# A second level of seven products for M4, stored weight sums, and merged down sums in an FNet and GeGLU kernel

## The chip, the cores and the metric

The kernel runs on one core of a Trainium2 chip. The metric is the device time of one execution in microseconds (us). Three runs of the kernel before gave 794.04, 794.16 and 794.77 us, a median of 794.16.

## What is computed

The input x has 2048 tokens of 512 features. It is normalised (layer norm), and two branches and the input are added:

```python
xn = layernorm(x)
# branch A: FNet, the real part of a 2-D DFT by matrices
a = xn @ dft_hid_re.T ; b = xn @ dft_hid_im.T
A = dft_seq_re @ a - dft_seq_im @ b
# branch B: gated GeGLU, 512 -> 1792 -> 512
B = (gelu(xn @ w_gate) * (xn @ w_up)) @ w_down
out = x + A + B
```

All of it is float32. A float32 matmul is made of three matmuls of a faster type (fp32r): each operand is split into a high part (a rounded copy, on ScalarE) and a low part (the difference, on VectorE), and high times high, low times high and high times low are added in PSUM (`mm3`). So every operand costs one ScalarE and one VectorE operation, the "split".

## The kernel before

Branch A and the preparation of the operands fill the time up to about 380 us (the first product of unit 0 starts at 379.8) and are not touched; the last products of branch A are fillers in the first units. Branch B is worked on in 28 *units* n. Even units make the gate of a block of 256 hidden features, odd units its up projection. Units 0 to 13 take the first half of the tokens (1024), units 14 to 27 the second half with the same weights, so weight block n and weight block n + 14 are the same. I call them the first and the second pass.

**Seven products.** A unit's product, weights (512 x 256) by tokens (512 x 1024), is split into two by two blocks and computed with seven block products in place of eight (the Strassen-Winograd scheme). They are numbered r = 0 to 6; product 0 is M1, product 4 is M4. Product r needs a sum of weight blocks or a plain block (`wl[n, r]`) and the same of token blocks (`xT[pass, r, i]`, i the two halves of the contraction). The weight sums are four VectorE operations on half tiles per unit (`weight_sums`, line 847), their splits are `weight_split`: three full tiles and a half. Each product is two `mm3`, six matmuls of 128 x 128 by 512 (`product`, `mult`). A unit uses three PSUM banks: a (products 0 and 1), b (5, 6, 3) and c (4, 2), with copies of intermediate sums between them: a to b, b to q6, b to w (`copy`, line 1993), and c added to w and q6 (`sums`, line 1997). PSUM has eight banks of this size.

**A second level for product 0.** From unit 4 on, product 0 of the units n and n + 1 (n even: 4, 6, 8, 10, 12) is computed for both passes at once: two weight blocks, two token halves and two halves of the contraction are again two by two blocks, so seven inner products of three matmuls each (`inner`, `inner_p`) give the four results. Those of the first pass go on in their units. Those of the second pass are completed in side tiles (q2, w2), written to DRAM by POOL (`m_park`), and loaded again in the second pass, where ScalarE copies them into the banks a and b in place of product 0 (`fetched`, the seeds sa and sb). The inner products need their own sums of tokens (`inner_x`, four once) and of weights (`inner_w`, four quarter operations per pair, line 911).

**Down projection.** Two units make one block q of hidden features (14 in all, 7 per pass): gelu of the gate, times the up projection, four tiles; four more sums (`h_sum`) and seven splits prepare them for the down projection, which is also done with seven products (`down_product`, per product r and output half j three matmuls per block). Blocks are taken in *turns*: in each pass first one block, then two, two and two. After a turn's product, ScalarE copies the bank to a tile `part` (line 2034) and POOL adds that tile onto `partial` in DRAM with an accumulating DMA (line 2036). A turn has 14 such steps (seven products, two halves). They are spread over the units as fillers: `fill` puts one at the fixed places d(0) to d(3) in a unit's order of products, and PE works on them while the copies of the unit are made. Just before the last blocks, two of the seven sums are added in SBUF by VectorE instead (line 2027). The very last turn (blocks 12 and 13) is `last_down`, an order written by hand that runs after everything else: it takes the parked sums as seeds in PSUM, adds the last products, combines them and stores.

**Operands of the second pass.** The tokens of the second half are prepared (sums and splits, `sum_x`, `xT_split`) while units 2 to 13 run, at units given by `X_UNIT`; seven of the resulting pairs of tiles (`PARK`) are written to DRAM and fetched later, to save SBUF.

**The order of the work.** Units 2 to 27 are ordered by a planner (`Plan`), a list scheduler that runs when the kernel is built: every operation is added with its engine, a cost (V5 = .6, V2 = .333 for VectorE on a full and a half tile, A5 = .52 and A2 = .31 for ScalarE, MM = .2267 per matmul), what it comes after, the tiles that it makes and uses, and the banks that it holds. PE's order is the order in which products are added. From PE's clock every other operation gets a due time, and then each engine takes what can start first. Loads on SP start at most `FETCH_AHEAD` = 16 before they are due, and operations that make tiles at most `EARLY` = 16. SBUF is 109 slots of 128 x 512 float32, of which the planner uses 107. Each engine, and the DMA queues of SP and POOL, then work strictly in that order, each instruction waiting for its operands.

Of the kernel before, what the change touches and what calls it, by code (L numbers as in the profile page):

```python
# [14 lines left out]
P = 128  # L15
S = 2048
D = 512
# [19 lines left out]
class Plan:  # L37
# [6 lines left out]
    def __init__(self, clocks, live, cap, ahead, early=LATE):  # L44
        self.early, self.had = early, set()
# [9 lines left out]
    def add(self, name, engine, cost, fn, after=(), makes=(), uses=(), due=None, mb=0, banks=(), holds=(), adds=False, begin=0.):  # L55
# [5 lines left out]
        self.ops[name] = dict(e=engine, cost=cost, fn=fn, after=after, makes=dict(makes), due=due, mb=mb, adds=adds, begin=begin, banks=tuple(banks), drains=bool(holds) and engine != "p")  # L61
# [48 lines left out]
    def choose(self, ready, frees, spare):  # L110
        best = None
        for e, names in ready.items():
            able = []
            for n, at in names.items():
                o = self.ops[n]
                at = max(at, self.clock[e], o["begin"])
                if e == "s":
                    at = max(at, o["due"] - self.ahead)
                elif o["makes"] and not o["begin"]:
                    at = max(at, o["due"] - self.early)  # L120
# [110 lines left out]
def fnet_geglu_kernel(ctx: ExitStack, tc: tile.TileContext, x, xt, cs, dh, wgu, wd, out):  # L231
# [81 lines left out]
    m_park = dram.tile([NP, P, CH], F32, name="m_park")  # L313
# [542 lines left out]
    def weight_split(n, k):  # L856

        if k == 3 or (k == 0 and fetched(n)):
            p, src = (3, wx[n][3][:, 0]) if k else (1, wx[n][0][:, 1])
            wl[n, p] = hl_half("w")  # L860
            return wl[n, p], src
# [20 lines left out]
    LEAD = 4  # L882

    def lead(n):
        return n % 2 == 0 and LEAD <= n < NP

    def fetched(n):
        return isinstance(n, int) and n >= NP + LEAD

    m0, xi, wi = {}, {}, {}  # L890

    def inner_x(k):

        b11, b21 = (xr[0, i, 0] for i in range(2))
        b12, b22 = (xr[1, i, 0] for i in range(2))
        u, v = {6: (b22, b12), 4: (b12, b11), 5: (b22, xi.get(4)), 3: (b21, xi.get(5))}[k]
        xi[k] = slot("xi")
        nc.vector.tensor_sub(xi[k], u, v)

    def inner_xsplit(k):  # L900
        xi["hl", k] = hl_tile(f"xi{k}")
        return xi["hl", k], xi[k]

    def inner_w(n, k):

        a, b = (wx[m][0][:, 0] for m in (n, n + 1))
        if k == 0:
            wi[n] = slot("wi", F32, (P, 4, P))
        op, u, v = ((OP.add, b[:, :P], b[:, P:]), (OP.subtract, wi[n][:, 0], a[:, :P]), (OP.subtract, a[:, :P], b[:, :P]),
                    (OP.subtract, a[:, P:], wi[n][:, 1]))[k]  # L910
        nc.vector.tensor_tensor(wi[n][:, k], u, v, op=op)

    def inner_wsplit(n):
        wi["hl", n] = slot("wih", F32R, (P, 4, P)), slot("wil", F32R, (P, 4, P))
        return wi["hl", n], wi.pop(n)

    def inner(n, k, ps, first=False):

        if k in (0, 1):
            a, b = [t[:, cols(k)] for t in wl[n, 0]], xT[0, 0, k]  # L920
        elif k == 3:
            a, b = [t[:, cols(1)] for t in wl[n + 1, 0]], xi["hl", 3]
        else:
            a, b = [t[:, {4: 0, 5: 1, 6: 2, 2: 3}[k]] for t in wi["hl", n]], xi["hl", k] if k != 2 else xT[1, 0, 1]
        mm3(ps, a, slice(P), b, first, True, resumed=not first)
# [78 lines left out]

    def last_down(qs):


        sp = NC // 2 - 1
        bank, p0 = {}, {}

        def add(dst, r, j, blk=None):
            nc.vector.tensor_add(dst, bank[r, j], dst)
            if blk:
                store(sp, blk[0], j, blk[1], dst)

        steps = [(r, j) for r in D_ORDER for j in range(2)][:-1]
        halves = [slice(h * HD, (h + 1) * HD) for h in range(2)]
        todo = steps + [(3, 1, h) for h in range(2)]

        def seed():  # L1020
            if todo:
                r, j, *h = k = todo.pop(0)
                sl = halves[h[0]] if h else slice(CH)
                bank[k] = ps_tile("dn")[:, :HD if h else CH]
                nc.scalar.activation(bank[k], acc[r, j][:, sl], AF.Copy)

        seed()
        seed()
        yield
        while carry:  # L1030
            carry.pop(0)()
        seed()
        for k in range(4):
            h_sum(NP - 1, k)
        seed()
        parts = [h_split(NP - 1, k) for k in (1, 0, 2, 3)]
        for r, j in steps:
            ps = bank[r, j]
            down_product(qs, r, j, ps, True)
            if r == 0:  # L1040
                p0[j] = slot("p0")
                nc.scalar.activation(p0[j], ps, AF.Copy)
            elif r == 2:
                nc.scalar.activation(acc[2, j], ps, AF.Copy)
            elif r == 1:
                nc.vector.tensor_add(acc[1, j], ps, p0[j])
                store(sp, 0, j, 0, acc[1, j])
            elif r == 5:
                add(p0[j], 5, j)
                nc.vector.tensor_add(acc[2, j], acc[2, j], p0[j])  # L1050
            elif r == 4:
                add(acc[2, j], 4, j, (0, 1))
            elif r == 6:
                add(p0[j], 6, j)
                nc.vector.tensor_add(acc[4, j], bank[4, j], p0[j])
                store(sp, 1, j, 1, acc[4, j])
            elif r == 3:
                add(p0[j], 3, j, (1, 0))
            seed()
            if parts and (r, j) != steps[0]:  # L1060
                split(*parts.pop(0))
        for h, (sl, queue) in enumerate(zip(halves, (nc.scalar, nc.sync))):
            down_product(qs, 3, 1, bank[3, 1, h], True, sl)
            nc.vector.tensor_add(p0[1][:, sl], bank[3, 1, h], p0[1][:, sl])
            queue.dma_start(out[3, 2 * sp, :, sl], p0[1][:, sl])
# [79 lines left out]
    def unit(n):  # L1145
# [49 lines left out]
        if fetched(n):  # L1195
            for t in (b, a):
                nc.scalar.activation(t, m0[n], AF.Copy)
        else:
            multiply(0, a, True)
            nc.scalar.activation(b, a, AF.Copy)  # L1200
# [624 lines left out]
    EARLY = 16  # L1825
    FETCH_AHEAD = 16
    PARK = [(0, 0), *((k, i) for k in (1, 4, 5) for i in range(2))]

    def middle():

        plan = Plan(dict(p=.3, v=6.6, a=4.2, s=0., g=0.), 84, SLOTS - 2, FETCH_AHEAD, EARLY)
        plan.idle = [0.] * 5 + [1., 1.5, 2.]
        add, W = plan.add, 6 * MM
# [6 lines left out]
        def split_of(key, f, ready, uses, makes, wide=True, **kw):  # L1840
# [5 lines left out]
            add(("lo", key), "v", V5 if wide else V2, lambda: split_lo(*begun.pop(key)), after=[("hi", key)], uses=[*uses, *makes])  # L1846

        def weights(m, load=True, sums=True, splits=True):
            if load:
# [389 lines left out]
```

## Time and profile before

| | |
|---|---|
| median of three runs | 794.16 us |
| the profiled execution's own time | 794.38 us |
| its span, first to last instruction | 792.6 us |
| PE, share of the span | 99%, 3468 matmuls |
| VectorE (DVE) | 92% |
| ScalarE (ACT) | 67% |
| GpSimd (POOL) | 21% |
| unit 2 begins | 404.7 us |
| unit 14 begins (second pass) | 583.1 us |
| last product of unit 27 ends | 769.6 us |

The profile is one execution. PE is TensorE's matmuls, PEld its weight loads, DVE VectorE, ACT ScalarE, POOL GpSimd and SP the engine that issues most DMAs (SPq is its queue). A row of a group gives line, engine, operation, output and inputs with their shapes, how often (x), then busy time in us and the mean in ns, then the idle time of the engine in front of it and who ended it. A row of waits gives the waiting engine and line, the releaser, the sum in us, how often, and the longest. A row of the chain gives start, length and what ran.

### The profile page before, as it was taken

To read this page: it belongs to the slowest core of one execution; us is meant where nothing else is said; L and a number is where in the kernel's file an instruction comes from. 1 tells how busy PE (TensorE), PEld (TensorE's weight loads), DVE (VectorE), ACT (ScalarE), POOL (GpSimd) and SP (SyncE) were. 2 spreads that over 40 slices of the span, in tenths; PEclk is the share of its full clock that TensorE was granted. 3 is DMA by queue.
4 is the path that set the end of the run, shared out by engine and by line. 5 is a ranking of instruction groups with operands and counts; after the bars stand their busy time and mean duration, and the time that the engine had idled before them with its cause. 6 is when DMAs were issued, how large, how long until landed. Compare 5 with 4: busy or idle time off the path is not lost.

```text
span 792.6 us, 11549 instructions
## 1 busy us (share of the span) xinstructions
PE 787.7 (99%) x3468; PEld 648.7 (82%) x3468; DVE 731.9 (92%) x1364; ACT 534.4 (67%) x1016; POOL 168.2 (21%) x242
## 2 busy tenths in 40 slices
PE   9999999999999999999999999999999999999998
PEld 6888888888888888888878888888888888888886
DVE  7999999999899979899999798999898889889897
ACT  6997656556534656366666876686876788777774
POOL 0110520044211231000202522422222234202220
PEclk9999999999999999999999999999999999999999
DMA  9967997879998897778725985966987799958972
GB/s 325 378 175 223 346 355 256 271 263 316 357 336 312 310 290 289 245 267 296 195 67 72 256 150 94 260 113 99 284 233 156 196 183 228 283 127 201 218 146 107
DMA packets 96432, 183.78 MB, mean 232 GB/s; under 512 B 11217, under 2 KB 18929, under 8 KB 96177
## 3 DMA queue, kind: packets, MB, share of 16 engines
q1 hardware_dynamic: 69840, 120.89, 44.9%
q0 software_dynamic: 26240, 61.88, 36.2%
q8 instruction: 27, 0.44, 0.2%
q14 instruction: 37, 0.29, 0.1%
q10 hardware_dynamic: 288, 0.26, 0.1%
HBM read 118.23 MB, written 67.91 MB: 235 GB/s over the span
## 4 chain that ended last, share of the span: by engine, by line
PE 90%; DVE 6%; DMA 1%; ACT 1%; issue 1%; ACTq 0%; DVEq 0%
PE m L280 33%; PE dn L280 17%; PE b L280 15%; PE c L280 10%; PE y L280 6%; PE a L280 5%; PE z L280 4%; DVE wl L269 1%; DVE ws L847 1%; DVE xr L780 1%; DMA dl<-d_park 1%; DMA wd<-in_wd 0%; DVE xr L781 0%; DMA x<-in_x 0%; DVE psl L269 0%
## 5 line engine op out<-in xcount | busy, mean ns | idle before, releaser
L264 ACT ACTIVATE psh<-pan 128x512 fp32r<-128x512 f32 x203 | 115.4, 625 | 72.4 <-DVE pan L660 26.4
L269 DVE TENSOR_TENSOR psl<-pan,psh 128x512 fp32r<-128x512 f32 x198 | 127.8, 684 | 8.9 <-ACT psh L264 8.2
L2036 POOL DMA_DIRECT2D partial<-part x94 | 81.8, 893 | 217.2 <-ACT part L2034 165.0
L280 PE MATMUL m<-psh,xcl 128*128 128x512 f32 x232 | 90.3, 389 | 0.0
L280 PE MATMUL m<-psl,xch 128*128 128x512 f32 x232 | 90.3, 389 | 0.0
L280 PE MATMUL m<-psh,xch 128*128 128x512 f32 x232 | 90.3, 389 | 0.0
L2034 ACT ACTIVATE part<-dn 128x512 f32<-128x512 f32 x94 | 55.2, 597 | 35.6 <-PE dn L280 33.1
L269 DVE TENSOR_TENSOR wl<-ws,wh 128x512 fp32r<-128x512 f32 x84 | 56.7, 685 | 3.1 <-ACT wh L264 3.0
L264 ACT ACTIVATE wh<-ws 128x512 fp32r<-128x512 f32 x84 | 51.1, 625 | 4.4 <-DVE ws L847 4.1
L280 PEld LDWEIGHTS m<-psh,xcl 128*128 128x128 f32 x232 | 43.5, 188 | 9.1
L280 PEld LDWEIGHTS m<-psl,xch 128*128 128x128 f32 x232 | 43.6, 188 | 9.0
L280 PEld LDWEIGHTS m<-psh,xch 128*128 128x128 f32 x232 | 43.6, 188 | 9.0
L581 POOL DMA_DIRECT2D partial<-part x28 | 21.0, 803 | 111.6 <-DMA bst<-mean_rstd 61.9
L269 DVE TENSOR_TENSOR htl<-s,hth 128x512 fp32r<-128x512 f32 x56 | 37.4, 686 | 3.3 <-ACT hth L264 3.1
L280 PE MATMUL m<-psh,xa 128*128 128x512 f32 x116 | 40.4, 389 | 0.0
L653 DVE TENSOR_TENSOR pan<-pan 128x512 f32<-128x512 f32 x58 | 37.9, 682 | 0.0
L957 DVE TENSOR_TENSOR s<-s 128x512 f32<-128x512 f32 x56 | 36.8, 685 | 0.1
L264 ACT ACTIVATE hth<-s 128x512 fp32r<-128x512 f32 x56 | 33.9, 625 | 2.6 <-DVE s L957 2.5
L280 PE MATMUL dn<-hl,wh 128*128 128x512 f32 x84 | 32.8, 390 | 0.0
L280 PE MATMUL dn<-hh,wh 128*128 128x512 f32 x84 | 32.7, 389 | 0.0
L280 PE MATMUL dn<-hth,wh 128*128 128x512 f32 x84 | 32.7, 389 | 0.0
L280 PE MATMUL dn<-hth,wl 128*128 128x512 f32 x84 | 32.7, 389 | 0.0
(850 smaller groups left out, 2317.9 us busy)
## 6 DMA issues: line engine op xcount, KB each, us to landing
pan<-in_cs SPq DMA_DIRECT2D x157, 256.0 KB, 5.4
partial<-part POOLq DMA_DIRECT2D x122, 256.0 KB, 5.4
wx<-in_wgu SPq DMA_DIRECT2D x56, 256.0 KB, 4.4
t_park<-pan POOLq DMA_DIRECT2D x29, 256.0 KB, 5.5
pan<-t_park SPq DMA_DIRECT2D x29, 256.0 KB, 4.5
wd<-in_wd SPq DMA_DIRECT2D x28, 256.0 KB, 5.2
acc<-partial SPq DMA_DIRECT2D x28, 256.0 KB, 5.3
zr<-z_park SPq DMA_DIRECT2D x16, 256.0 KB, 3.6
```

What stands on the lines that cost most here:

```text
L264: nc.scalar.activation(t[0], src, AF.Copy, scale=float(sign))
L269: engine.tensor_sub(t[1], src, hi)
L280: nc.tensor.matmul(ps, a[u][:, sl], b[v], start=first and r == 0, stop=last and r == 2, skip_group_check=resumed)
L581: nc.gpsimd.dma_start(partial[sp, r, j], ypart.pop((r, j)), **({} if r in (0, 5, 6) else {"accum_op": OP.add}))
L653: return [lambda: nc.vector.tensor_sub(t3, b22, b12), lambda: nc.vector.tensor_sub(t1, b12, b11), lambda: (nc.vector.tensor_sub(b22, *((t1 ...
L780: nc.vector.tensor_sub(v, v, xst[sp, t, 0])
L847: nc.vector.tensor_tensor(r[k][:, h], u, v, op=op)
L957: nc.vector.tensor_sub(t, u, v)
L2034: nc.scalar.activation(part[0], tiles[j], AF.Copy)
L2036: add(("da", qs[-1], r, j), "g", .6, lambda j=j, part=part: nc.gpsimd.dma_start(partial[sp, r, j], part[0], accum_op=OP.add), after=[("dc" ...
```

## The change

- **M4.** Product 4 gets the second level too, for the four pairs that begin with units 6, 8, 10 and 12 (`LEAD = {0: 4, 4: 6}`). The functions of the inner level take the outer product r (0 or 4) as a parameter. In units 20 to 27 bank c is seeded by a third ScalarE copy. Two more banks are held in a pair unit. Both lists of inner token sums start two units ahead (`INNER_AHEAD`).
- **Weight sums stored.** Units 4 to 13 write their two tiles of weight sums to DRAM (`ws_park`, on POOL). Units 18 to 27 load them (`load_sums`) instead of computing them, and load only the two half tiles of raw weights that are products themselves (`load_short`), as one tile whose split is one operation. From unit 20 on, the half that product 4 would need is neither loaded nor split.
- **Turns.** The turns are `TURNS`: one block, then pairs through blocks 9 and 10, and three for the last turn (11, 12, 13), so the second pass has turns of 2, 2 and 3 in place of 1, 2, 2 and 2. Block 7 goes with block 8, and all 14 steps of a turn are taken one half at a time. Steps are spread evenly over the units up to the next turn (`wanted`).
- **The last turn** is added to the planner, step by step, in place of the hand-written order.
- **Order and settings.** A unit's order of products is given by a string (digits are products, d0 to d3 fillers, X and Y inner products of this and the pair before). Look-ahead: 28 for operations that make tiles, 22 for loads, 12 for raw weights before unit 12. Two input sums of the second half (k = 6 and 3) are also written to DRAM and read back (`x_park`), the splits of k = 2 are added to `PARK` and half of k = 4 taken out, and the units of the splits change.

```diff
-    LEAD = 4
+    LEAD = {0: 4, 4: 6}
+    LATER = {0: False, 4: False}
+    KEEP_SUMS = (4, NP)
...
+    def short(n):
+        return fetched(n, 0) and n >= NP + KEEP_SUMS[0]
+
+    def half_split(n, k):
+        return k == 3 or (k < 2 and fetched(n, 4 * k) and not (k == 0 and short(n)))
...
-    EARLY = 16
-    FETCH_AHEAD = 16
-    PARK = [(0, 0), *((k, i) for k in (1, 4, 5) for i in range(2))]
+    HURRY = 28
+    LOOSE = 15
+    LATER_HURRY = 28
+    FETCH_AHEAD = 22
+    W_AHEAD = 12
+    TURNS = [[0], [1, 2], [3, 4], [5, 6], [7, 8], [9, 10], [11, 12, 13]]
+    INNER_AHEAD = 2
+    INTO_ACC = (6, 3)
+    SUMS_AT = 3.5
+    PARK = [(0, 0), (4, 0), *((k, i) for k in (1, 5, 2) for i in range(2))]
...
+            if sums and at >= count + keep:
+                add(("sw", m, 3), "s", .9, lambda: load_sums(m, at - count, int(name == "d")), after=[("lw", m), ("pw", name, at - count)],
+                    mb=2 * MB if name or not fetched(m, 4) else 1.5 * MB, makes={("ws", m, 0): 1, ("ws", m, 1): 1}, uses=[("wx", m)])
+            elif sums:
                 box = []
+                if keep <= at < count:
+                    add(("pw", name, at), "g", 1.2, lambda: park_sums(m, at, int(name == "d")),
+                        after=[("sw", m, 3)], uses=[("ws", m, 0), ("ws", m, 1)], mb=2 * MB)
...
+        def park_sums(m, at, d):
+            for i in range(2):
+                nc.gpsimd.dma_start(ws_park[d, at, i], wx[m][1 + i].rearrange("p a b -> p (a b)"))
+
+        def load_sums(m, at, d):
+            t = [slot("ws", F32, (P, 2, HD)) for _ in range(2)]
+            for i in range(2):
+                some = slice(1 - i if fetched(m, 4) else 0, 2)
+                nc.sync.dma_start(t[i][:, some], ws_park[d, at, i].rearrange("p (a b) -> p a b", a=2)[:, some])
+            wx[m] = (wx[m][0], *t, wx[m][-1])
...
-        X_UNIT = {0: 2, 1: 3, 4: 8, 5: 9, 2: 11, 6: 12, 3: 12}
+        X_UNIT = {0: 2, 4: 5, 1: 3, 5: 8, 2: 9, 6: 12, 3: 12}
...
+        def order(n):
+            if lead(n, 4):
+                return "X00 X40 d1 X01 X41 X04 5 1 X05 d2 6 X06 X44 d0 3 X03 X02 X45 2 d3 X46"
+            if lead(n, 0):
+                return "X00 4 X01 d1 5 1 d2 X04 6 X05 d0 3 X06 d3 2 X03"
+            if lead(n - 1, 4):
+                return "5 Y43 1 d1 Y42 d2 6 d0 3 d3 2"
+            if lead(n - 1, 0):
+                return "4 Y02 d1 5 1 d2 6 d0 3 d3 2"
+            if fetched(n, 4):
+                return "5 1 d2 6 d0 3 d1 2 d3"
+            if fetched(n, 0):
+                return "4 d1 5 1 d2 6 d0 3 d3 2"
+            return "0 4 d1 5 1 d2 6 d0 3 d3 2"
...
+            wanted = -(-len(todo) // (turn - n))
...
+                if u[0] == "d":
+                    for _ in range((wanted - int(u[1]) + 3) // 4):
+                        fill()
...
+                sent = [("da", qs[0] - 1, r, j)] if qs[0] % (NP // 2) else [("lys", j, 1)] if sp and r == 3 else []
                 add(("da", qs[-1], r, j), "g", .6, lambda j=j, part=part: nc.gpsimd.dma_start(partial[sp, r, j], part[0], accum_op=OP.add),
-                    after=[("dc", qs[0], r, j)], uses=[("part", qs[0], r, j)], mb=MB, adds=True)
+                    after=[("dc", qs[0], r, j), *sent], uses=[("part", qs[0], r, j)], mb=MB, adds=True)
...
+        def last_down(qs):
+
+            sp, tiles, p0 = NC // 2 - 1, {}, {}
+            given = TURNS[-2]
+
+            def step(r, j, *h):
+                k, sl = (r, j, *h), slice(h[0] * HD, (h[0] + 1) * HD) if h else slice(CH)
+                hold, a = ("dn", "z", *k), ("acc", 2, r, j)
+
+                def seed():
+                    tiles[k] = ps_tile("dn")[:, :HD if h else CH]
+                    nc.scalar.activation(tiles[k], acc[r, j][:, sl], AF.Copy)
+                add(("zs", *k), "a", A2 if h else A5, seed, after=[("la", 2, r, j), ("dc", given[0], r, j)], uses=[a], banks=[hold], holds=[hold])
+                w = {0: 0, 1: 0, 4: 1, 5: 1, 6: 2, 2: 2, 3: 3}[r]
+                add(("z", *k), "p", (1.5 if h else 3) * MM * len(qs), lambda: down_product(qs, r, j, tiles[k], True, sl),
+                    after=[("zs", *k)] + [("lo", ("w", ("d", q), w)) for q in qs] + [("lo", ("h", q, r)) for q in qs],
+                    uses=[("wl", ("d", q), w) for q in qs] + [("hl", q, r) for q in qs], holds=[hold])
...
+        hidden_sums(NP - 1)
+        last_down(TURNS[-1])
```

More of the change, by code (lines that the diff above doesn't have):

```diff
@@ L53, in done, with add @@
         self.ends[name] = at
-    def add(self, name, engine, cost, fn, after=(), makes=(), uses=(), due=None, mb=0, banks=(), holds=(), adds=False, begin=0.):
+    def add(self, name, engine, cost, fn, after=(), makes=(), uses=(), due=None, mb=0, banks=(), holds=(), adds=False, begin=0., ahead=None):
         after = list(after)
@@ L1991, in f @@
                 else:
[L1992 to L1997 removed]
+                    side[(n, to, *more)] = slot(to)
```

474 lines of the change are left out of this document (251 added, 223 removed).

## The prediction

> **What bounds the kernel now.** I read the page first, then the waits of PE, then the chain.
>
> ```profile
> span 792.6 us, 11549 instructions
> PE 787.7 (99%) x3468; PEld 648.7 (82%) x3468; DVE 731.9 (92%) x1364; ACT 534.4 (67%) x1016; POOL 168.2 (21%) x242
> ...
> q1 hardware_dynamic: 69840, 120.89, 44.9%
> q0 software_dynamic: 26240, 61.88, 36.2%
> ```
> ```profile
> PE warm L1274 <- PEq L2232: 0.8, 1, 0.8
> PE b L280 <- ACT w L1993: 0.3, 1, 0.3
> ```
> ```profile
> 439.77 1.36 PE dn L280 x6
> ...
> 769.57 19.29 PE dn L280 x90
> ```
>
> PE is busy for 99% of the span, and in the whole program it waits once on another engine, for 0.3 us. A busy PE need not be at its peak, so I check the pace: six matmuls take 1.36 us in the chain, 0.2267 us each, and 3468 of them make 786 us. There is no slack between matmuls: the time is the number of matmuls, and each one more or less counts, as long as the others keep PE fed. VectorE at 92% is the next candidate, so I cut the planned part into stages: units 2 to 13 (404.7 to 583.1), 14 to 19, 20 to 27, and the last turn of down sums. The columns are: window, PE, PEld, DVE, ACT, POOL, clock, DMA share, GB/s.
>
> ```profile
> 100.00:200.00 100.00, 100.00 (x442) 82.79 (x442) 98.85 (x169) 58.66 (x103) 24.02 (x40) 1.00 0.89 294
> 404.70:432.80 28.10, 27.81 (x121) 22.36 (x120) 27.88 (x56) 18.22 (x35) 4.44 (x6) 1.00 0.27 34
> 404.70:583.10 178.40, 178.11 (x785) 146.80 (x784) 163.46 (x319) 131.63 (x249) 51.16 (x67) 1.00 0.74 164
> 583.10:666.20 83.10, 83.10 (x368) 68.83 (x367) 72.97 (x142) 61.35 (x121) 22.47 (x26) 1.00 0.85 181
> 666.20:769.60 103.40, 103.40 (x458) 85.63 (x457) 95.34 (x183) 78.17 (x153) 23.42 (x27) 1.00 0.86 204
> 769.60:788.90 19.30, 19.25 (x90) 15.76 (x89) 17.70 (x30) 10.89 (x22) 0.00 (x0) 1.00 0.19 74
> ...
> 664.80:690.70 25.90, 25.90 (x116) 21.46 (x115) 23.61 (x45) 20.12 (x40) 8.61 (x10) 1.00 1.07 260
> ```
>
> Two rows serve as yardsticks. From 100 to 200 us VectorE is 98.85% busy and PE loses nothing; from 404.7 to 432.8 it is 99.2% busy (27.88 of 28.10) and PE loses 0.29. In the last row the DMA share is 1.07 and PE is full. The clock is 1.00 in every row.
>
> **PE.** Product 4 of units n, n+1, n+14, n+15 is four times 6 matmuls; the inner seven are 7 x 3 = 21. Four groups save 4 x 3 = 12 matmuls, 12 x 0.2267 = 2.72 us. Nothing else in the change alters the count: down steps are merged, not dropped. The matmuls move, though. The first pass gains 4 x (21 - 12) x 0.2267 = 8.2 us (178.4 to 186.6). Units 20 to 27 lose their product 4 (8 x 1.36) and 8 of 28 down steps: 60 steps of 1.36, 81.6 us. Units 14 to 19 have 62 steps, 84.3 us. The last turn takes 14 x 9 matmuls, 28.6 us.
>
> [...]
>
> **VectorE.** Durations:
>
> ```profile
> L1997 DVE TENSOR_TENSOR q<-c,q 128x512 f32<-128x512 f32 x16 | 10.9, 684 | 0.0
> L269 DVE TENSOR_TENSOR wil<-wi,wih 128x512 fp32r<-128x512 f32 x5 | 3.4, 686 | 0.0
> L911 DVE TENSOR_TENSOR wi<-wx 128x128 f32<-128x128 f32 x10 | 2.8, 285 | 0.0
> L898 DVE TENSOR_TENSOR xi<-xr 128x512 f32<-128x512 f32 x2 | 1.4, 684 | 0.0
> L269 DVE TENSOR_TENSOR xi4l<-xi,xi4h 128x512 fp32r<-128x512 f32 x1 | 0.7, 685 | 0.0
> ```
> ```profile
> L269 DVE TENSOR_TENSOR wl<-ws,wh 128x512 fp32r<-128x512 f32 x24 | 16.1, 687 | 1.2 <-ACT wh L264 1.2
> L269 DVE TENSOR_TENSOR w<-wx,w 128x256 fp32r<-128x256 f32 x14 | 5.9, 420 | 0.1
> ...
> L847 DVE TENSOR_TENSOR ws<-wx 128x256 f32<-128x256 f32 x12 | 5.0, 419 | 0.0
> ```
>
> Added, all in the first pass: four input sums and four splits (8 x 0.685), and per group four quarter sums (4 x 0.285), a split (0.686) and two bank sums (2 x 0.684): 5.5 + 4 x 3.19 = 18.3 us. So 163.5 + 18.3 = 181.8 us in 186.6, 97.4%. Removed for units 18 to 27: four half sums each (10 x 4 x 0.419 = 16.8), two half splits that become one (10 x (0.840 - 0.687) = 1.5), and for units 20 to 27 a full split that becomes a half (8 x 0.267 = 2.1): 20.4 us. The rows of 666.2 to 769.6 hold six units' sums (x12, two a unit) and seven units' half splits (x14), so 13.0 of the relief falls there: 95.3 - 13.0 = 82.3 us against PE's 81.6, 101%. The stage before it drops to 73.0 - 7.4 = 65.6 in 84.3 (78%), and the last turn has 28.6 for some 17.7. The look-ahead grows from 16 to 28 us, a good unit more; a unit's weights are three splits (1.8) and half a down block (four half sums, three splits and a half, 4.2/2), so about 4.5 us moves forward out of units 20 to 27, which leaves 95%. Over all three stages and the last turn VectorE has 347.7 us in 381.1, 91%, as before.
>
> What PE loses to this: nothing by the row at 98.85%, or 0.29 per 28.1 us by the row at 99.2%, which over 186.6 + 81.6 us is 2.8. Both stretches lie nearer the first row; I take two waits, 0.6.
>
> **ScalarE, PSUM.**
>
> ```profile
> L2034 ACT ACTIVATE part<-dn 128x512 f32<-128x512 f32 x94 | 55.2, 597 | 35.6 <-PE dn L280 33.1
> ```
> ```profile
> L264 ACT ACTIVATE wih<-wi 128x512 fp32r<-128x512 f32 x5 | 3.1, 627 | 0.0
> ...
> L1993 ACT ACTIVATE b<-b 128x512 f32<-128x512 f32 x5 | 2.9, 582 | 3.4 <-PE b L280 3.3
> ```
>
> Added per group: three copies (0.58 to 0.60) and a split (0.627), and four input splits once: 4 x 2.4 + 2.5 = 12.1 us in the first pass, 131.6 + 12.1 = 144 of 186.6 (77%). In the second pass eight seeds of bank c (8 x 0.6 = 4.8) against 14 copies of down sums dropped (14 x 0.597 = 8.4); the three seeds that now open units 20 to 27 take 1.8 us, and after product 6 of the unit before they have at least products 3 and 2 and a down step (4.1) to hide in. The tightest new cover is in unit n+1, where inner product 3 stands one product (1.36) behind inner product 6 and needs its copy (0.6). Every unit already covers the copy of w by one step in the same way, and of 26 units one waited, the 0.29 of 416.3. So: free to 4 x 0.29; I take nothing beyond the 0.6. Banks: a pair unit holds a, c, b and three for the inner sums, six of eight.
>
> **Queues.**
>
> ```profile
> L1951 SPq DMA_DIRECT2D m<-m_park x10: 319/327/438, 603.1 to 721.6; - x10
> L2140 POOL DMA_DIRECT2D m_park<-w x5: 551/573/573, 449.0 to 568.7; - x5
> ...
> DMA to landing us min/median/max: 2.3/4.4/10.0
> ```
> ```profile
> L2036 POOL DMA_DIRECT2D partial<-part x94 | 81.8, 893 | 217.2 <-ACT part L2034 165.0 <-ACT w L264 15.4 <-ACT s L939 13.6
> ```
> ```profile
> POOL partial L2036 <- DMA partial<-part: 9.4, 3, 4.7
> ```
>
> POOL issues 20 parks of sums, 8 of M4, 4 of input sums and 2 more of input splits: 34 x 0.57 = 19 us on 51 in the first pass (38%). Behind a park that waits for its sum stand accumulates, for which only buffers and later loads wait; POOL idles 217 us ahead of them. In the second pass 14 accumulates go (14 x 0.893 = 12.5). SP issues as many more loads, 34 x 0.33 = 11 us over 380. The new loads are asked for up to 22 us ahead, and the raw weights of the first pass 12 instead of 16; parks and loads of this kind landed within 10.0, so both are still in time. The order now asked of accumulates on one block costs nothing new: they waited for each other before, three times, and only POOL stood. Bytes: 40 transfers of 0.262 MB more in the first pass; at q1's price (0.449 x 792.6/120.89 = 2.94 us a MB) 31 us on 132, a share of 0.87. In the second pass 3.7 MB more (11 us) less 14 accumulates at q0's 4.64 us a MB (17 us). The row at 1.07 covers both; a load that misses its unit would cost up to its landing time, 10.0; I take zero, because PE's waits show none on a DMA.
>
> **Last turn.**
>
> ```profile
> 770.58 0.19 PEld L280 LDWEIGHTS dn<-hl,wh 128*128 128x128 f32 x1 [0.30 <-DVE hl L269]
> ...
> 788.89 0.42 DVE L1064 TENSOR_TENSOR p<-dn,p 128x256 f32<-128x256 f32 x1 [0.18 <-PE dn L280]
> ```
>
> Its first step now has six matmuls of two finished blocks ahead of the one that waited here, so 0.3 goes; it could also stay. The end (last half sum, store) is the same work: 3.7 us from the last matmul to the end of the span.
>
> **The sum** is made against the profiled execution, 794.38 us, whose span is 792.6: 794.38 - 2.72 - 0.3 + 0.6 = 791.96. It lies 0.22 above the median of 794.16, so 791.7.
>
> **Rivals.**
> - *VectorE sets the pace in units 20 to 27 (slower).* For: 82.3 us of its work against 81.6 of PE, and in that stage it idled 103.4 - 95.3 = 8.1 us before, in places fixed by the order of the queue. Where nothing is done ahead and that idle stays, the stage takes 90.4, 8.8 more: 800. That decides from 4.0 us of the 8.8 on (791.7 + 4.0 = 795.7); with half of it, 4.4, the time is 796.1. Against: 18.7 us of VectorE are free in the stage before and 11 behind it. Chance 0.18.
> - *The first pass gives the gain back (no change).* The idle of 14.9 us shrinks to 4.8; if a fifth of the 10.1 is missing, 791.7 + 2 = 793.7. For: the planner's cost of such an operation, V5, is 0.6, and it takes 0.685, so VectorE runs behind its plan in a full stretch. Against: the row at 98.85%. Chance 0.09.
> - *Banks run short in the four pair units (no change).* With six held, a down step gets its bank only when ScalarE has drained the one before: 0.6 for each of four units, 2.4 in all, 794. [...] Chance 0.04.
> - *VectorE's total is the bound everywhere (no change).* Its work shrinks by 2 us only, but the matmuls removed would bring nothing: 794.2. [...] Against: PE is full while VectorE idles 8%. Chance 0.03.
>
> **How the numbers follow.** The forecast has 0.66: 791.7, with its own range of 790.8 (both old waits gone and no new one: 794.16 - 2.72 - 0.6) to 792.5. About 0.2% (1.6 us) is what a measurement of this kernel can tell from no change, so under 792.6 is faster and over 795.7 slower. No change holds 0.09 + 0.04 + 0.03 = 0.16, slower 0.18. The range reaches from 790.8 over the cases of no change to 795.8 and leaves out the slower one.
>
> **What would show it.** Right: 12 matmuls fewer, PE waits under 1.5 us in all, units 20 to 27 in some 82 us, the last turn in 28.6 and no wait at its start; VectorE at 95% or more in the first pass and at about 90% in the second. Wrong: waits of PE products on VectorE (w, wl, hl) or on copies, bunched in units 6 to 13 or 20 to 27, or on dn banks in units 6, 8, 10 and 12.

## The result and the profile after

| | before | after | forecast |
|---|---|---|---|
| median, nine runs each on one chip | 794.3 us | 792.3 us | 791.7 us |
| its runs (forecast: the range) | 794.04 to 794.8 | 791.89 to 793.3 | 790.8 to 795.8 |
| ratio to before, 95% interval | | 0.9974 (0.9964 to 0.9985) | |
| profiled execution | 794.38 us | 792.34 us | 791.96 us |
| its span | 792.6 us | 790.6 us | |

The kernel became 2.0 us faster, 0.26%. The forecast was 2.5 us. First the page of the kernel after: span and engines.

```profile
span 790.6 us, 11662 instructions
...
PE 785.8 (99%) x3459; PEld 647.0 (82%) x3459; DVE 730.4 (92%) x1350; ACT 538.8 (68%) x1020; POOL 175.6 (22%) x262
```

Nine matmul records fewer stand there for twelve matmuls fewer, because one step of the last turn is computed in two halves in both kernels: its 9 matmuls on three blocks make 18 records, where 6 on two blocks made 12 (x135 for 14 x 9 = 126 in the row of the last turn below, x90 for 84 in the chain of before). VectorE's busy time is again 92% of the span.

Then the stages of the kernel after, with the columns of the prediction's table. The cuts are where unit 2, unit 14, unit 20, the last turn and the end of the last matmul lie.

```profile
404.90:592.40 187.50, 186.98 (x821) 153.35 (x820) 179.39 (x356) 143.35 (x272) 71.38 (x102) 1.00 0.85 212
592.40:676.70 84.30, 84.30 (x374) 69.80 (x373) 72.16 (x131) 60.24 (x115) 18.45 (x22) 1.00 0.92 224
676.70:758.50 81.80, 81.80 (x362) 67.75 (x361) 68.98 (x123) 67.71 (x131) 14.67 (x17) 1.00 0.85 218
758.50:787.20 28.70, 28.62 (x135) 23.88 (x133) 27.29 (x48) 14.89 (x29) 0.00 (x0) 1.00 0.16 64
```

PE is full in the second pass and the last turn. What is left to lose lies in the first pass: it holds 819 matmuls, 819 x 0.2267 = 185.64, and lasts 187.48 us, so PE stands 1.84. Before, 783 matmuls (177.48) took 178.40, so it stood 0.92. The difference of the two spans, 2.0 us, then comes out as follows.

| term | us |
|---|---|
| 12 matmuls x 0.2267 | -2.72 |
| standing of PE in the first pass, 0.92 to 1.84 | +0.92 |
| units 14 to 27, beside their matmuls | 0.00 |
| last turn, beside its 42 matmuls more (19.16 to 28.55 from its first matmul's start to its last one's) | -0.13 |
| end, from the start of the last matmul (4.04 to 3.73) | -0.31 |
| up to unit 2 (404.69 to 404.89), work that the change doesn't touch | +0.19 |
| sum | -2.05 |

The waits of PE in the kernel after (who waits, for whom, us in all, times, longest):

```profile
PE warm L1225 <- PEq L2340: 0.8, 1, 0.8
PE b L280 <- ACT q L2007: 0.4, 1, 0.4
```

There is one wait on an engine in this list, for ScalarE's copy to q. With the slower first matmul behind it, it costs 0.7 us (the matmul starts 0.60 late and the next one 0.11).

That is less than half of the 1.84. Most of the rest is in no row of PE, because a matmul's row lasts 0.39 us and the next one starts 0.2267 after it: a standing of up to 0.16 leaves no gap between the rows. The waits of the weight loads in the first pass show it (this list holds the wait for q as well):

```profile
PEld b L280 <- ACT q L2007: 1.1, 2, 0.9
PEld b L280 <- ACT w L2007: 0.9, 2, 0.4
PEld b L280 <- ACT b L2007: 0.5, 1, 0.5
```

By the starts of the matmuls PE loses 0.29, 0.32 and 0.28 us at 430.3, 437.5 and 457.5, and 0.10 at 413.4 (before: 0.23 at 413.0 and 0.57 at 416.3, where the list has 0.3). Each time a product waits for a copy by ScalarE. At 437.5 and 457.5 the copy starts as soon as its bank is done, and all that covers it is a down step of one block, three matmuls or 0.68 us:

```profile
436.86 0.58 ACT L2007 ACTIVATE b<-a 128x512 f32<-128x512 f32 x1
...
437.49 0.19 PEld L280 LDWEIGHTS b<-xT50h,wh 128*128 128x128 f32 x1 [0.47 <-ACT b L2007]
```

These two are too little cover. At 430.3 the copy stood in ScalarE's queue behind a split that had waited 0.55 us for VectorE.

The chain shows what stands behind the wait at 514; here the columns are start, length and what ran:

```profile
506.07 7.23 DMA partial<-part
514.03 4.38 PE b L280 x18
...
758.45 28.68 PE dn L280 x135
```

The chain is PE up to 462 us and again from 514.03. In between it runs over ScalarE and POOL, and the last long piece there is a DMA. It is the accumulate of a down sum, issued by POOL at 506.07 and landed 7.23 us later, at 513.30. ScalarE waits for it, by the timeline around that place and by its own list of waits:

```profile
513.38 0.60 ACT L2007 ACTIVATE q<-b 128x512 f32<-128x512 f32 x1 [1.02 <-DMA partial<-part]
...
514.03 0.50 PE L280 MATMUL b<-xi46h,wih 128*128 128x512 f32 x1 [0.44 <-ACT q L2007]
```
```profile
ACT q L2007 <- DMA partial<-part: 1.0, 1, 1.0
```

So the path is: the copy to q gets an SBUF slot that held a `part` tile; the accumulating DMA still reads that tile; ScalarE works in order, so it stands 1.02 us in front of the copy; and PE, whose next matmul overwrites bank b, waits for the copy. In the kernel before ScalarE waits on no DMA between 404 and 760 us.

### The profile page after: what moved, and what is told of

The parts are those of the page before. It is cut to its first block, busy times and chain, and to the rows that moved or that the text cites. A ratio compares the mean times of both kernels' runs of the same rounds, so it can differ in the third digit from the quotient of the medians.

```text
span 790.6 us, 11662 instructions
## 1 busy us (share of the span) xinstructions
PE 785.8 (99%) x3459; PEld 647.0 (82%) x3459; DVE 730.4 (92%) x1350; ACT 538.8 (68%) x1020; POOL 175.6 (22%) x262
## 4 chain that ended last, share of the span: by engine, by line
PE 93%; issue 3%; POOL 2%; DMA 1%; ACT 1%; DVE 0%; POOLq 0%; ACTq 0%
PE m L280 35%; PE b L280 16%; PE dn L280 15%; PE y L280 10%; PE c L280 7%; PE a L280 6%; PE z L280 4%; POOL partial L2096 1%; DMA partial<-part 1%; PE warm L1225 1%; POOL ws_park L1848 0%; POOL m_park L2015 0%; ACT b L2007 0%; POOL xT_hl L822 0%; ACT wh L264 0%
## 5 line engine op out<-in xcount | busy, mean ns | idle before, releaser
L2096 POOL DMA_DIRECT2D partial<-part x80 | 70.7, 892 | 175.7 <-ACT part L2093 151.8
L2093 ACT ACTIVATE part<-dn 128x512 f32<-128x512 f32 x80 | 47.3, 593 | 22.3 <-PE dn L280 21.1
L269 DVE TENSOR_TENSOR wl<-ws,wh 128x512 fp32r<-128x512 f32 x76 | 51.2, 685 | 4.0 <-ACT wh L264 3.8
L264 ACT ACTIVATE wh<-ws 128x512 fp32r<-128x512 f32 x76 | 46.1, 624 | 3.4 <-DVE ws L849 3.3
L583 POOL DMA_DIRECT2D partial<-part x28 | 21.0, 797 | 95.0 <-DMA bst<-mean_rstd 61.9
L264 ACT ACTIVATE hh<-s 128x512 fp32r<-128x512 f32 x42 | 25.9, 627 | 11.5 <-DVE s L961 11.5
L280 PE MATMUL dn<-hh,wl 128*128 128x512 f32 x84 | 32.7, 389 | 0.0
```

The costliest lines, as they stand in the source:

```text
L264: nc.scalar.activation(t[0], src, AF.Copy, scale=float(sign))
L269: engine.tensor_sub(t[1], src, hi)
L280: nc.tensor.matmul(ps, a[u][:, sl], b[v], start=first and r == 0, stop=last and r == 2, skip_group_check=resumed)
L583: nc.gpsimd.dma_start(partial[sp, r, j], ypart.pop((r, j)), **({} if r in (0, 5, 6) else {"accum_op": OP.add}))
L2093: nc.scalar.activation(part[0], tiles[j], AF.Copy)
L2096: add(("da", qs[-1], r, j), "g", .6, lambda j=j, part=part: nc.gpsimd.dma_start(partial[sp, r, j], part[0], accum_op=OP.add), after=[("dc" ...
```

## The experiments

All times are medians, and each ratio is to the kernel before on the same chip in the same job. My theory after the result had two parts: the gain is the matmuls of M4, and the loss against them is ScalarE standing for a slot in unit 8. The rivals were that the stored sums or the turns carry part of the gain, that VectorE's full stretch causes the loss, and that the order of products in the pair units does.

### M4 taken out, all else kept

```diff
-    LEAD = {0: 4, 4: 6}
+    LEAD = {0: 4}
```

> The changed kernel without the second level for M4; stored sums, turns, last turn and look-ahead stay. Theory (the time is the matmuls plus PE's waits): 12 matmuls come back, 792.3 + 2.7 = 795.0, less what of the 0.9 us of new waits in units 2 to 13 belongs to the M4 pairs, so 794.1 to 795.0. Rival (VectorE sets the pace): the first pass loses 18 us of VectorE work, so the time does not rise: 792.3 or less.

Measured: 794.21 us (793.86 to 794.54), ratio 0.9998 (0.9989 to 1.0007). Its first pass and the waits of its PE on engines:

```profile
404.87:583.38 178.51, 178.45 (x784) 146.66 (x783) 164.80 (x323) 133.45 (x253) 66.34 (x94) 1.00 0.86 213
```
```profile
PE warm L1225 <- PEq L2340: 0.8, 1, 0.8
```

With the rest of the change in place, the whole gain is M4's: without it nothing measurable is left, and the two intervals (to 0.9985 with it, from 0.9989 without) do not overlap. M4 brings 1.9 us (794.21 - 792.3) of the 2.72 that its matmuls are worth. The wait at 514 is gone with it, and PE stands 1.03 us in the first pass (178.51 less 783 x 0.2267) in place of 1.84. The stands at 430.3, 437.4 and 457.5 are still there, so they are not M4's. POOL still issues 94 instructions in the first pass against 67 in the kernel before, and that alone makes no wait of PE's list.

### Stored weight sums taken out

```diff
-    KEEP_SUMS = (4, NP)
+    KEEP_SUMS = (NP, NP)
```

> The changed kernel with the weight sums of units 18 to 27 computed again instead of stored and loaded. VectorE gets 10 x 1.67 + 1.5 = 18 us back in units 14 to 27: 141 + 18 = 159 of 166 us, 96%; 40 DMAs go. Theory: VectorE's slack in units 14 to 19 and the longer look-ahead hide nearly all of it, 792.3 to 793.3. Rival (my slower case: VectorE bound in units 20 to 27): PE waits for VectorE there, 795 to 800.

Measured: 792.98 us (791.68 to 794.72), ratio 0.9983 (0.9974 to 0.9992). Units 14 to 27 of this kernel, then its waits:

```profile
592.40:676.70 84.30, 84.30 (x374) 69.82 (x373) 78.86 (x156) 61.18 (x121) 18.66 (x22) 1.00 0.90 218
676.70:758.50 81.80, 81.80 (x363) 67.75 (x362) 76.48 (x152) 68.21 (x137) 14.77 (x17) 1.00 0.81 208
```
```profile
PE b L280 <- ACT q L2007: 1.6, 1, 1.6
```
```profile
ACT w L264 <- DMA xT_hl<-xT51h: 1.9, 1, 1.9
...
ACT q L2007 <- DMA xT_hl<-xT51l: 0.6, 1, 0.6
```

VectorE has 14.2 us more to do in units 14 to 27 (78.86 + 76.48 against 72.16 + 68.98), is 93.5% busy from unit 20 on, and PE is full all the same. The stored sums relieve an engine that wasn't late. Against the kernel after it is 0.7 us longer, which the two intervals don't separate. In the profiles its spans differ by 0.5 and the wait at the end of unit 8 by 1.1 (514.87, 1.75 in place of 0.60): there ScalarE stands for slots that the *parks* of operands (`xT_hl`) still read. The cause is of the same kind, with another DMA.

### Turns as before: 1, 2, 2 and 2 in the second pass

```diff
-    TURNS = [[0], [1, 2], [3, 4], [5, 6], [7, 8], [9, 10], [11, 12, 13]]
+    TURNS = [[0], [1, 2], [3, 4], [5, 6], [7], [8, 9], [10, 11], [12, 13]]
```

> The changed kernel with the second pass's turns as before (1, 2, 2, 2), the last turn of two blocks still planned. Matmuls are the same; 14 copies and 14 accumulates come back, 9.5 us of PE move from the last turn to the units. Theory: all of it is off the path except the 0.3 us wait that the first step of a short last turn had: 792.3 to 792.8. Rival (accumulates hold the SBUF slots that other operations wait for): waits on accumulates appear in units 14 to 27, 793.5 to 795.

Measured: 803.94 us (803.75 to 804.3), ratio 1.0121 (1.0107 to 1.0134). The largest waits of PE, and three stretches around them:

```profile
PE dn L280 <- DVE wl L269: 2.5, 1, 2.5
PE dn L280 <- ACT wh L264: 2.0, 1, 2.0
PE b L280 <- ACT q L2007: 1.2, 1, 1.2
PE dn L280 <- ACT dn L2213: 1.1, 1, 1.1
```
```profile
698.00:720.00 22.00, 22.00 (x99) 18.23 (x98) 15.25 (x25) 16.27 (x32) 3.49 (x4) 1.00 0.84 224
720.00:740.00 20.00, 15.56 (x58) 12.13 (x58) 18.59 (x35) 15.45 (x31) 3.51 (x4) 0.83 1.01 259
732.00:737.00 5.00, 4.82 (x12) 3.82 (x13) 4.43 (x8) 3.11 (x7) 0.88 (x1) 0.52 1.05 381
```

This is the miss of the study: I had priced the turns at nothing beside the 0.3 at the start of the last one. With the old turns in the new order, the weights of turn (10, 11) are asked for by 710.3 and land at most 6.3 us after that, but their sums are made only at 728.5 to 731.4 and their splits at 731.4 to 733.9, when PE already stands at the first step. In the 22 us before, VectorE is 69% busy (15.25 of 22.00). It isn't short of time; its order puts the work late. This is the mechanism of my first rival, at one turn of another order. Whether the old turns are dearer in any order, or only in the one that the list scheduler happens to give them here, I can't tell apart.

### Costs of the scheduler set to the measured ones

```diff
+    V5, V2, A5, A2 = .685, .42, .6, .41
```

> The changed kernel whose planner counts the measured times (0.685 and 0.42 for VectorE, 0.60 and 0.41 for ScalarE on full and half tiles) in place of 0.6, 0.333, 0.52, 0.31. Theory (PE's 1.8 us of waits in units 2 to 13 come from copies that queue behind other ScalarE work because the plan undercounts): waits shrink to under 1 us, 791.4 to 792.0. Rival (they come from SBUF slots and landing accumulates, or from too little cover): 792.3 or more, and the order of the queue changes elsewhere for the worse.

Measured: 813.23 us (811.67 to 814.81), ratio 1.0242 (1.0228 to 1.0256). The two largest waits of PE:

```profile
PE dn L280 <- DVE acc L2087: 5.2, 1, 5.2
PE dn L280 <- DVE w L269: 3.7, 1, 3.7
```

Prices nearer to the profile gave the worst order of all: preparation comes too late for down steps at 767.9, just before the last product of unit 27, and at 800.6, in the last turn. So the optimistic V5 of my second rival doesn't show as a defect here, and better prices did not make a better order. Experiments that change the whole order therefore carry this scatter, and I read them by their waits, not by their sum.

### Another order of products in the pair units of M4

```diff
-    "X00 X40 d1 X01 X41 X04 5 1 X05 d2 6 X06 X44 d0 3 X03 X02 X45 2 d3 X46"
+    "X00 X40 d1 X01 X41 X04 5 1 X05 d2 6 X06 X44 X45 d0 3 X03 X02 2 d3 X46"
...
-    "5 Y43 1 d1 Y42 d2 6 d0 3 d3 2"
+    "5 1 Y43 d1 Y42 d2 6 d0 3 d3 2"
```

> The changed kernel with inner product 5 of M4 moved ahead of product 3 and inner product 3 moved behind the next unit's product 1, so that the copies of M4's bank have two or more products to hide in. If the wait of 0.44 us (with its tail 0.7) at the last inner product of unit 8 is one of too little cover: it goes, 791.6 and a span of 789.9. If the copy is late because its SBUF slot is still read by an accumulate (the trace names that DMA): the wait stays or moves, 792.3.

Measured: 793.66 us (793.07 to 795.83), ratio 0.9994 (0.9986 to 1.0003), 1.4 more than the higher of the two expected times. The largest wait of PE, VectorE's wait on a DMA in this pass, and ScalarE's in front of the late copy:

```profile
PE b L280 <- ACT w L2007: 1.8, 1, 1.8
```
```profile
DVE ws L849 <- DMA xT_hl<-xT51l: 3.2, 1, 3.2
```
```profile
522.01 0.63 ACT L264 ACTIVATE hh<-s 128x512 fp32r<-128x512 f32 x1 [3.11 <-DVE s L961]
```

More cover at this place only moved the loss: the wait at 514 went, and at 525.7 another of 1.8 came. Its way is longer. VectorE stands 3.16 us, until 516.14, for a slot that a park still reads, and works without a break from there to 522. ScalarE stands 3.11 us for the sum s that it makes, and the copy to w stands behind that. (ScalarE also stood 2.08 us for an accumulate, until 514.33, and PE did not wait then.) So a slot that a DMA still reads stands at the start of this wait too, and reaches PE by way of two engines. Cover decided where PE felt it.

### More work for VectorE, more work for ScalarE, in the first pass

Twenty splits of weights (units 5 to 14) are done twice. In the first kernel the low parts, on VectorE (20 x 0.685 = 13.7 us); in the second the high parts, on ScalarE (20 x 0.627 = 12.5 us). The result is the same.

```diff
                 split_lo(*t)
+                if again(key):
+                    split_lo(*t)
```

> The changed kernel with twenty low splits of weights (units 5 to 14, two each) done twice, unknown to the planner: 20 x 0.687 = 13.7 us more VectorE work in the first pass, where it idles 8.1 of 187.5 us. If VectorE's total decides: the stage cannot hold it, at least 5.6 us longer, 798 or more. If VectorE's lateness has slack (it is up to 28 us ahead of PE): 792.3 to 794.

> The same twenty, but the high splits on ScalarE: 20 x 0.624 = 12.5 us more there, where it idles 44 of 187.5 us. If a free share of an engine is what counts: nothing, 792.3 to 792.8, and less than the VectorE run. If PE's waits are copies that queue behind whatever ScalarE does just then: more and longer waits on copies, 793 to 796.

Measured: 797.74 us (797.37 to 799.06), ratio 1.0046 (1.0032 to 1.006) for VectorE; 794.56 us (794.22 to 796.82), ratio 1.0008 (0.9999 to 1.0017) for ScalarE. The first pass of each (187.48 us in the kernel after), with waits; VectorE doubled:

```profile
404.51:597.67 193.16, 188.55 (x820) 152.81 (x819) 190.04 (x375) 141.80 (x271) 71.19 (x102) 1.00 0.82 208
```
```profile
PE b L280 <- ACT w L2015: 2.8, 3, 1.6
PE b L280 <- ACT q L2015: 1.7, 1, 1.7
```

ScalarE doubled:

```profile
404.35:595.09 190.74, 187.36 (x821) 153.25 (x820) 178.71 (x356) 153.71 (x292) 71.18 (x102) 1.00 0.84 210
```
```profile
PE b L280 <- ACT q L2012: 1.9, 1, 1.9
...
PE b L280 <- ACT w L2012: 0.8, 1, 0.8
PE b L280 <- ACT b L2012: 0.7, 1, 0.7
```

VectorE is idle for 187.5 - 179.4 = 8.1 us in the first pass of the kernel after. Adding 13.7 costs 5.4 us, close to the 5.6 that don't fit (13.7 - 8.1): the kernel after has little room left on VectorE there. But ScalarE, idle for 44 us (187.5 - 143.35), isn't free either: 12.5 us on it cost 2.3. In both kernels PE waits for copies by ScalarE to b, q and w, and never for VectorE's low parts. Work that VectorE or ScalarE does elsewhere shows up as a late copy, since the copies stand in ScalarE's queue. Part of both costs is the wait of unit 8 again, which grows from 0.60 us to 1.84 (at 516.75) and 2.10 (at 515.64), with ScalarE standing 1.3 and 1.6 us for an accumulate just before. So of the 2.3 us some 1.5 are a slot, and only the rest copies behind doubled splits (0.84 us at 437.6, where the kernel after has 0.21, and 0.92 at 584.0). That 5.4 comes so near to 5.6 may be chance.

### Look-ahead back to 16 us

```diff
-    HURRY = 28
-    LATER_HURRY = 28
-    FETCH_AHEAD = 22
+    HURRY = 16
+    LATER_HURRY = 16
+    FETCH_AHEAD = 16
```

> The changed kernel with the look-ahead of before (16 for operations that make tiles and for loads). If the longer look-ahead is what lets VectorE carry units 20 to 27 (its work there is 82 us by the old order against 81.6 of PE): PE waits for splits there, 795 to 800. If the slack of the stage is enough without it: 792.3 to 793.

Measured: 800.41 us (799.85 to 800.59), ratio 1.0075 (1.0059 to 1.009). Units 20 to 27 and the last turn, and the largest wait of PE:

```profile
676.70:758.50 81.80, 81.80 (x363) 67.73 (x362) 64.71 (x119) 65.58 (x130) 14.81 (x17) 1.00 0.87 238
758.50:795.00 36.50, 31.05 (x137) 25.34 (x136) 33.95 (x58) 18.88 (x37) 0.00 (x0) 0.95 0.13 50
```
```profile
PE dn L280 <- DVE w L269: 4.2, 1, 4.2
```

The look-ahead matters by 8.1 us, but not where my first rival had it. From unit 20 to 27 PE stays full, and VectorE does less there (64.7 us) than in the kernel after (69.0); the rest falls into the last turn, where VectorE is 93% busy and PE stands 5.5 of 36.5 us.

### The slot: four ways to remove or to feed the wait in unit 8

Each changes what holds slots around 514 us; the first has the scheduler take a DMA to end 2.5 us after its bytes have moved and not 0.7. The last one is a version I hoped would beat both.

```diff
+        plan.LAND = 2.5
```
```diff
-        plan = Plan(dict(p=.3, v=6.6, a=4.2, s=0., g=0.), 84, SLOTS - 2, FETCH_AHEAD, HURRY)
+        plan = Plan(dict(p=.3, v=6.6, a=4.2, s=0., g=0.), 84, SLOTS - 6, FETCH_AHEAD, HURRY)
```
```diff
-    LEAD = {0: 4, 4: 6}
+    LEAD = {0: 4, 4: 4}
```
```diff
-        X_UNIT = {0: 2, 4: 5, 1: 3, 5: 8, 2: 9, 6: 12, 3: 12}
+        X_UNIT = {0: 2, 4: 5, 1: 3, 5: 9, 2: 10, 6: 12, 3: 12}
```

> The changed kernel whose planner takes every DMA of units 2 to 27 to land 2.5 us after its bytes have moved, not 0.7, so that it hands a slot on later once a park or accumulate has read it. If PE's wait in unit 8 comes from ScalarE standing for a slot that a park or accumulate still reads: ScalarE's waits on DMAs vanish, PE's waits in the first pass fall from 1.8 to 1.1 or less, 791.5. If the wait is a matter of cover or of ScalarE's share: no lower than 792.3. Either way the whole order shifts, which by the runs so far can cost several us elsewhere.

> The changed kernel whose planner may use 103 of the 109 slots instead of 107. Slots held by parks: every slot has rested longer when it is used again, ScalarE does not stand for DMAs, 791.5 to 792.3, unless four slots fewer push the preparations of a later stage together (as in the run with less look-ahead): then 795 to 800.

> The changed kernel with M4's second level from unit 4 on, five pairs. Three matmuls fewer, 0.7 us: 791.6, if PE's waits stay. The fifth pair adds 3.2 us of VectorE work to units 4 and 5 and brings 5.5 us of input sums and splits forward, where VectorE is already at 26.8 of 27.1 us: if VectorE's total decides there, 793 to 796.

> The changed kernel with the splits of input product 5 (whose tiles are parked) begun in unit 9 instead of 8, and those of 2 in unit 10 instead of 9, so that fewer parks stand in front of unit 8's end. Slots held by parks: the wait at the end of unit 8 goes, 791.6, or reappears one unit later, 792.3 to 793. Cover: it stays at its place.

| edit | median (runs) | ratio, 95% interval |
|---|---|---|
| DMAs taken to end later | 795.87 (794.81 to 797.06) | 1.002 (1.0011 to 1.0029) |
| four slots fewer | 797.38 (796.28 to 798.72) | 1.0038 (1.0025 to 1.0052) |
| M4 in five groups | 800.53 (799.09 to 801.61) | 1.0071 (1.0056 to 1.0086) |
| splits of two token sums one unit later | 791.24 (791.09 to 791.76) | 0.9961 (0.9948 to 0.9973) |

First the last one. It takes two splits of tokens and the four parks behind them (`xT_hl`, k = 5) out of unit 8 into unit 9 and later, with two sums that are written to DRAM (`x_park`), and those of k = 2 into unit 10 and later. The first pass and the waits of PE:

```profile
404.44:591.16 186.72, 186.66 (x820) 153.50 (x819) 178.19 (x356) 143.04 (x272) 71.18 (x102) 1.00 0.84 212
```
```profile
PE warm L1225 <- PEq L2340: 0.8, 1, 0.8
PE z L280 <- DVE xa L370: 0.2, 1, 0.2
```

The wait at 514 is gone, and ScalarE waits on no DMA from 404 to 760 us. VectorE and ScalarE have nearly the same work in the first pass as in the kernel after (178.19 and 143.04 against 179.39 and 143.35), so neither engine's load over the pass caused the wait. The stands at 429.9, 437.0 and 457.1 are still there (0.26, 0.32 and 0.28 us). The median is 1.06 us lower than that of the kernel after, more than the wait's 0.7: the first pass is 0.76 shorter, and another 0.4 of its profile lies in the part up to unit 2, which no edit touches. It beats both kernels by its median, and all its runs lie below all of the kernel after; the two intervals against the kernel before overlap.

The other three remove this wait or move it, and pay elsewhere. With DMAs taken to end later, 0.5 us is left of PE's standing between 480 us and the end of the first pass, but ScalarE still stands 1.5 once for a `partial`, which I expected to vanish, and waits of 1.3 (in two pieces) and 2.06 us appear at 749 to 750.5 and 762. With four slots fewer ScalarE waits on no DMA, but the preparation bunches: the listed waits are 2.0 at 761.8 and 1.3 at 531.7. M4 in five groups should save another 0.68 us (3 matmuls x 0.2267) and is 8.2 longer than the kernel after, above both expectations. Its largest wait of PE (the next, 2.5 us, lies in the last turn), and ScalarE's:

```profile
PE b L280 <- ACT q L2007: 2.7, 1, 2.7
```
```profile
ACT q L2007 <- DMA xT_hl<-xT51h: 2.5, 1, 2.5
```

At the end of unit 8 it has the same wait in its largest form: the copy to q stands 2.5 us for a slot that a park reads, and PE 2.7.

## Why the prediction was right, and where it was off

- **PE as the bound, 12 matmuls, 2.72 us.** Right. Without M4 the time is that of before. (No run here has a plain float32 matmul of this size, so that fp32r is the faster type is not shown; the sum uses only the 0.2267 us measured for it.) The sign I named, waits under 1.5 us in all, holds by PE's list (1.2 with the 0.8 of the start) but not by the starts of the matmuls (1.84 in the first pass). The stages have the forecast lengths: 187.5, 84.3, 81.8 and 28.7 us against 186.6, 84.3, 81.6 and 28.6. The first is longer by the 0.92 us that PE stands more.
- **The last turn.** It runs 28.68 us in the chain without a wait, as forecast, but it saves 0.13 us and not 0.3. The 0.30 was the wait of a weight load; behind it the matmul started 0.03 late and the next one 0.11, so 0.14 was there to save. The end is 0.31 shorter, which I had as unchanged, and nothing here shows why. The two errors go opposite ways.
- **"I take two waits, 0.6", on VectorE.** The size is near (the first pass stands 0.92 more), the place and cause are not, so the nearness is luck. PE waits for copies by ScalarE. Nearly all of the 0.92 is 0.71 for a slot in unit 8 and 0.99 at the four smaller stands, less the 0.80 of the two stands before. The price of 0.29 a wait was also too low: the wait listed with 0.3 at 416.3 cost PE 0.57.
- **The steps that failed are "Queues" and the covers of copies.** I priced late accumulates and parks at nothing because "only buffers and later loads wait" for them. What I left out: the buffer is next written by ScalarE, whose queue is in order and holds the copies that free PSUM for PE. So an accumulate for which ScalarE stood 1.02 us reached PE although PE waits on no DMA. This kernel showed it once, for 0.7 us; six variants have the same wait at the end of unit 8 (listed with 1.1 to 2.7 us at 514.6 to 518.8), each behind ScalarE standing for a DMA. And I took copies as covered by a step of PE: a down step of one block is 0.68 us, a copy 0.58 plus its start, and that costs 0.3 at 437.5 and at 457.5.
- **VectorE, stage by stage.** The total is right (347.8 us, forecast 347.7, or 347.4 when its own terms are added), the first pass nearly (95.7% against 97.4%). The split of the second pass is wrong: units 20 to 27 have 69.0 us and not 77.8 (the 82.3 less the 4.5 moved ahead), and the last turn 27.3 and not 17.7. I moved work ahead by the look-ahead only; the scheduler also left about 10 us of it for the last turn, which is now 95% busy on VectorE. That it didn't cost anything there is this order's luck: with a shorter look-ahead it costs.
- **Turns priced at 0.3.** Not borne out as a separate price. In this order the old turns cost 11.6 us. Part of that is a halved clock (0.52 in the row from 732 to 737), and how much belongs to the turns themselves stays open.
- **Rivals.** VectorE as the pace of units 20 to 27: falls for this kernel (PE full at 84%, and still full at 93.5% without the stored sums); its mechanism, preparation bunched ahead of a down step, is what other settings ran into, in the turn at 729 or in the last turn. The first pass giving the gain back: it gave back 0.92 of the 2.0 I had named, through copies and not through VectorE's total, and the run with more work on VectorE shows how close that is. Banks short in the pair units: no wait on a dn bank is listed for PE or for its weight loads in the first pass, so the four times 0.6 of this rival did not show. VectorE as the bound everywhere: falls, since 14 us of its work more in the second pass cost nothing there and 12 matmuls fewer brought 1.9 us. That it has little room in the first pass alone is shown by the doubled splits.

## What to carry to other kernels

In this kernel PE is full, 99% of the span, and the worth of the change was its matmuls: 1.9 us measured of the 2.72. In a kernel like it, look for the cost where a buffer changes hands (0.7 us here, behind ScalarE standing 1.02 us for an accumulate): ask who writes next into the slot that a DMA reads, and what else stands in that engine's queue. The idle time of an engine was no cover here: ScalarE idled 44 us of the first pass, and PE waited 0.60 us for its copy all the same. What counted was the place of the copy in the queue. And with a list scheduler, a part of a change can't be priced by taking it out alone, because the whole order moves (11.6 us for the turns that I had priced at 0.3); read such a run by its waits.

## What was not expected of the hardware

A wait of PE cost nearly twice its own length where the granted clock was lower behind it. A window of the kernel with four slots fewer, behind its wait of 2.1 us (2.0 in the list) at 761.8; then of the kernel with M4 in five groups, in and behind its wait that ends at 518.8; then of the kernel with DMAs taken to end later, behind its wait of 2.06 us at 762:

```profile
762.60:766.00 3.40, 3.40 (x10) 2.66 (x9) 3.40 (x7) 3.37 (x8) 0.00 (x0) 0.53 0.00 0
```
```profile
517.20:518.10 0.90, 0.00 (x0) 0.00 (x0) 0.90 (x3) 0.00 (x0) 0.90 (x1) 1.00 1.07 430
518.20:519.00 0.80, 0.19 (x1) 0.19 (x2) 0.75 (x2) 0.80 (x2) 0.00 (x0) 0.50 1.03 412
519.20:525.20 6.00, 6.00 (x15) 4.61 (x15) 3.81 (x9) 3.12 (x7) 1.63 (x3) 0.52 0.64 191
525.10:526.00 0.90, 0.90 (x6) 0.72 (x5) 0.80 (x3) 0.11 (x1) 0.00 (x0) 1.00 0.00 0
```
```profile
762.00:766.00 4.00, 4.00 (x17) 3.28 (x18) 4.00 (x7) 3.28 (x8) 0.00 (x0) 1.00 0.00 0
```

In the second block the granted clock is 1.00 in the row up to 518.1, 0.50 in the row from 518.2, 0.52 from 519.2 to 525.2 and 1.00 again in the last row. In the 6 us at 0.52, 15 matmuls start where 26 would at 0.2267 us each, so by this estimate 2.6 us are lost behind a wait of 2.8 (2.7 in the list); PE is "busy" for all of it, and only the clock (0.52) tells.

The length of a wait alone did not tell whether the clock would be lower behind it. Behind the 2.1 us at 761.8 it was 0.53. Behind the 2.06 us at 762 in the last row it was 1.00, and the first pass of the kernel with ScalarE's splits doubled has 1.00 with a wait of 2.10 us in it (at 515.64). What makes the difference, no run here shows.
